# Chunked attention and a two-expert router on one core: the same operations in a new planned order, with a longer instruction fetch in the planner and one more dependency for turned rows

## Chip, cores and metric

The kernel runs on one core of one Trainium2 chip. The metric is device time in microseconds (us) of one execution. The core has TensorE (PE, matmuls and their weight loads), VectorE (DVE), ScalarE (ACT), GpSimd (POOL, which also issues most DMAs) and SyncE (SP, which issues DMAs only).

## What is computed

Attention in chunks, then a mixture of experts on its rows. The reference, cut to what matters:

```python
# q, k, v: (4, 8, 768, 64); mem_k, mem_v: 8 memory rows per head
for c in range(768 // 32):                       # chunks of 32 queries
    k_full = concat(mem_k, k[16 before .. 8 behind the chunk])   # 64 rows; v alike
    a = softmax(q_c @ k_full.T / sqrt(64))
    out[chunk] = a @ v_full
x = out as (3072 tokens, 512)
logits = x @ w_gate + log1p(exp(x @ w_noise)) * noise            # 8 experts
top2 = the two best experts of each token; weights by softmax over the two
for e in range(8):
    out[tokens of e] += weight * (relu(x @ w1[e]) @ w2[e])       # 512 -> 1024 -> 512
```

## The kernel before

**Attention.** A *pair* is two heads of one batch element (here a *batch* is one of the four batch elements, 768 tokens); there are 16 pairs, four to a batch, and a *group* is two pairs whose q, k and v are loaded together. The operations of a pair, with the planner's labels: `tq` and `tk` turn q and k on PE; `eq` and `ek` copy them out of PSUM; `sc` makes the scores; on DVE `mx` takes their maximum and `sb` subtracts it (L592, L608); `ex` is the exponential on ACT (L611); `tp` turns it, `ep` copies it; `pvo` multiplies it with v (L631); `rc` and `ml` divide by the sum and write the rows (DVE, L635 and L647); `tx` and `exx` turn the rows for the router. Loads are DMAs that GpSimd issues: `lq`, `lk` (one each a group) and `lv` (two halves a group). `lm`, on SyncE, copies the memory rows of v into the same tile. The memory rows' source, `memv`, lies inside the tile `XS`, which later holds the turned rows of the experts. There are 3 buffers each for q, k and v of a group, one PSUM tile for scores and one for outputs.

**Router.** After four pairs a batch is routed: `lg` makes the logits on PE (L693), `r1` is softplus on ACT, `r2` on DVE chooses two experts of each token (the choice, `pk`, L707 to L722), `r3` on PE ranks the tokens by matmuls with a triangle (L735 to L739), `r3s` and `r6` give each token a slot (L749 to L772), `r4`, `r5`, `r7` make the gates (L759 to L760, L763, L903 to L907), `r8` and `r8a` build one-hot products (`ohv` at L744, on DVE or POOL; `ohl` at L786), `r9` (L793) sums them to a table of token numbers by slot, `s0` to `s3` and `stab` do the same for spare slots. The rows and gates are written to memory (L913, on SyncE). The labels of batch 2 end in `_s`, those of batch 3 in `_l`.

**Experts.** There are 28 tiles of tokens, one for each two experts. For experts 0 and 1 half of each tile is *sealed* once batch 2 is routed: its token numbers are final (`gid_s`, L807), and 7 gathers (L949) fetch its rows. `tt` turns gathered rows on PE (L980), `xev` copies them into `XS` (L368 or L370), `fo` is the first matmul of an expert, one for each 128 columns of the hidden layer (L1055; `fo_a` for sealed halves), `relu` follows (L1065, L1067), `so` is the second matmul (L1096), DVE or ACT weights and adds it (L1105 to L1115), and POOL scatters the sum to the output (L1127). After attention the remaining PSUM banks serve the experts.

**What sets the order.** Every operation is given to a planner with a list of engines and durations, the operations that it depends on, its buffers and a priority. `Planner.run` plays the program through and writes each engine's instructions in the order of its own start times; each engine then runs its instructions strictly in that order on the chip, and waits on the chip come from the tiles that an instruction reads and writes, not from the planner's dependencies. `SHIFT` adds a number to the priority of an operation by label or by label and count. `FETCH` describes the fetch of PE's instructions: blocks of 128 products, the first edge at 94, and 6.3 us from the start of one block to the time when the next one is there as long as the planned time is under 97, later 3.2 us. These lines hold it:

```python
            if o.mm:
                for edge in range(block + FETCH[0], products + o.mm + 1, FETCH[0]):
                    at = est + dur * (edge - products) / o.mm
                    stall = max(0.0, begun + (FETCH[2] if at < FETCH[3] else FETCH[4]) - at)
```

## Time and profile before

| | |
|---|---|
| time, 3 runs | 337.85, 338.81, 338.9 us (median 338.81) |
| the profiled execution | 333.6 us, of which the span from first to last instruction is 332.1 |
| PE busy | 282.3 us (85%), 2972 matmuls |
| weight loads | 177.1 us (53%) |
| DVE, ACT, POOL busy | 159.8, 147.9, 131.3 us |
| granted PE clock, mean | 0.903 |

Times in a profile are those of one execution. A timeline row has its start, its length, engine, line, operation, output and inputs, shapes, and in brackets the idle time before it with what ended that. A row of groups has busy time and the mean in ns of one instruction, then the idle time before such instructions. PEq and the like are an engine's sequencer.

### The profile page before, as it was taken

Reading aid. Unit: us, or ns where it says so; the run is one execution under the profiler, and the core shown is the slowest. Engines: PE = TensorE matmul, PEld = TensorE weight load, DVE = VectorE, ACT = ScalarE, POOL = GpSimd, SP = SyncE. Lnnn points to the kernel's source line nnn. Section 1 sums busy time; section 2 is a strip of 40 time slices with the busy share of each in tenths; the row PEclk is TensorE's granted clock in tenths of the full one; section 3 lists DMA queues with packets and bytes.
Section 4 is the critical chain, followed back from the end, with each engine's and each line's share of the span. In section 5 each row is a group of like instructions: output and inputs, shape, how many; then the busy total and the mean of one; then the engine's idle time right before and its main releaser. Section 6 shows DMA issues by size and latency. Waiting matters only on the chain.

```text
span 332.1 us, 7279 instructions
## 1 busy us (share of the span) xinstructions
PE 282.3 (85%) x2972; PEld 177.1 (53%) x2972; DVE 159.8 (48%) x372; ACT 147.9 (45%) x261; POOL 131.3 (40%) x178
## 2 busy tenths in 40 slices
PE   0587588777567679999999999999999999999991
PEld 0575366665446456664646655545545744744540
DVE  7776677888748776824313431144042041043041
ACT  8675667888264134760611417403703604603500
POOL 7767533345000776987282410132032032051072
PEclk9999975978755558999999999999999999999998
DMA  7999999999999359289999910699613621021032
GB/s 100 208 128 139 149 150 149 212 171 195 223 183 116 89 127 177 79 140 188 247 210 227 248 68 0 106 182 198 101 54 78 99 79 57 2 109 51 3 122 82
DMA packets 80013, 43.55 MB, mean 131 GB/s; under 512 B 53805, under 2 KB 73262, under 8 KB 79974
## 3 DMA queue, kind: packets, MB, share of 16 engines
q0 software_dynamic: 74672, 38.78, 100.2%
q1 hardware_dynamic: 5014, 4.19, 4.9%
q8 instruction: 24, 0.39, 0.5%
q14 instruction: 15, 0.12, 0.1%
q10 hardware_dynamic: 288, 0.07, 0.1%
HBM read 61.26 MB, written 10.85 MB: 217 GB/s over the span
## 4 chain that ended last, share of the span: by engine, by line
PE 59%; DMA 21%; issue 8%; POOL 4%; DVE 4%; ACT 1%; POOLq 1%; DVEq 0%; ACTq 0%
PE ps_l L1055 20%; DMA vg<-in_v_dram 19%; PE ps_l L1096 18%; PE ps_g L1096 7%; PE ps_g L1055 7%; PE ps_l L980 2%; POOL out_dram L1127 2%; PE ps_o L631 2%; DMA kn<-in_k_dram 2%; PE ps_g L656 1%; DVE xrow L647 1%; POOL vg L516 1%; POOLq L1183 1%; PE ps_g L617 1%; PE ps_s L585 1%
## 5 line engine op out<-in xcount | busy, mean ns | idle before, releaser
L1065 ACT ACTIVATE ht<-ps_l 128x384 bf16<-128x384 f32 (+2 forms) x110 | 48.5, 491 | 95.0 <-PE ps_l L1055 94.0
L1096 PE MATMUL ps_l<-w2l,ht 128*128 128x512 bf16 x328 | 73.7, 379 | 0.0
L1096 PEld LDWEIGHTS <-ht 128*128 128x128 bf16 x448 | 43.6, 98 | 51.5
L1127 POOL DMA_INDIRECT out_dram<-acc,oid x28 | 28.8, 1028 | 84.9 <-DVE acc L1115 79.7
L1115 DVE SCALAR_TENSOR_TENSOR acc<-ps_l,gates,acc 128x512 f32<-128x512 f32 x22 | 16.5, 751 | 60.3 <-PE ps_l L1096 59.3
L1055 PEld LDWEIGHTS <-w1t 128*128 128x128 bf16 x416 | 31.4, 100 | 19.6 <-issue 2.2
L1055 PE MATMUL ps_l<-XS,w1t 128*128 128x384 bf16 (+4 forms) x312 | 40.7, 285 | 0.7 <-ACT XS L368 0.7
L1055 PEld LDWEIGHTS <-w1l 128*128 128x128 bf16 x320 | 29.9, 98 | 19.1
L1055 PE MATMUL ps_l<-XS,w1l 128*128 128x512 bf16 (+3 forms) x240 | 39.9, 316 | 0.0
L516 POOL DMA_DIRECT2D vg<-in_v_dram x18 | 23.7, 1317 | 23.3 <-DMA vg<-in_v_dram 10.7
L368 ACT COPY kT<-ps_q 64x768 bf16<-64x768 bf16 x31 | 24.6, 793 | 8.8 <-PE ps_q L555 8.2
L1096 PE MATMUL ps_g<-w2l,ht 128*128 128x512 bf16 x120 | 28.2, 379 | 0.0
L555 PE MATMUL ps_q<-identb,qn 128*64 128x128 bf16 x192 | 11.9, 276 | 15.6 <-POOL identb masks.py:199 10.6
L631 PE MATMUL ps_o<-vg,PT 128*32 128x132 bf16 x384 | 12.1, 279 | 9.0 <-DMA vg<-in_v_dram 5.0
L1107 DVE TENSOR_SCALAR acc<-ps_l,gates 128x512 f32<-128x512 f32 x13 | 9.8, 751 | 19.6 <-PE ps_l L1096 19.6
L1065 ACT ACTIVATE ht<-ps_g 128x384 bf16<-128x384 f32 (+2 forms) x38 | 16.8, 471 | 5.3 <-PE ps_g L1055 5.1
L949 POOL DMA_INDIRECT xl<-x_rows,gid x16 | 16.7, 1044 | 5.8 <-PE ps_l L980 2.2
L555 PEld LDWEIGHTS <-qn 128*64 128x64 bf16 x192 | 9.6, 147 | 16.6 <-DMA qn<-in_q_dram 12.6
L592 DVE TENSOR_REDUCE mx<-ps_s 128x12 f32<-128x768 f32 x16 | 15.3, 953 | 3.8 <-PE ps_s L585 3.4
L368 ACT COPY PT<-ps_g 128x768 bf16<-128x768 bf16 x13 | 10.3, 796 | 12.3 <-PE ps_g L617 11.2
L961 DVE COPY gates<-xl 64x8 f32<-64x8 f32 (+1 forms) x40 | 11.0, 292 | 9.9 <-DMA xl<-x_rows,gid 8.0
L647 DVE TENSOR_TENSOR xrow<-ps_o,rec 128x768 bf16<-128x768 f32 x16 | 15.3, 958 | 0.6
(179 smaller groups left out, 387.7 us busy)
## 6 DMA issues: line engine op xcount, KB each, us to landing
w2l<-in_moe_w_dram POOLq DMA_DIRECT2D x8, 1024.0 KB, 11.2
vg<-in_v_dram POOLq DMA_DIRECT2D x14, 336.0 KB, 20.9
w1t<-in_moe_w_dram POOLq DMA_DIRECT2D x4, 1024.0 KB, 22.3
w1l<-in_moe_w_dram POOLq DMA_DIRECT2D x4, 1024.0 KB, 10.5
kn<-in_k_dram POOLq DMA_DIRECT2D x8, 384.0 KB, 15.0
qn<-in_q_dram POOLq DMA_DIRECT2D x8, 384.0 KB, 18.7
x_rows<-xrow SPq DMA_DIRECT2D x2, 792.0 KB
x_rows<-xrow SPq DMA_DIRECT2D x2, 768.0 KB
```

Of the source, the lines that this page charges most:

```text
L368: A.copy(dst, src)
L516: G_.dma_start(out=vt[p0 + j:p0 + j + nj, hh, c:c + n, :D], in_=bass.AP(v.tensor, v.offset + (hd * S + c * chunk + j - left_ctx) * D, [[D, ...
L555: P_.transpose(out=dst.t[64 * hh:64 * hh + 64, t * QP:(t + 1) * QP], in_=s[:, j + 2 * hh, t, :], identity=identb)
L592: mx = op("mx", ("DVE", 0.98), lambda o, bmx=bmx, bS=bS: V.tensor_reduce(out=bmx.t, in_=sv(bS), axis=AX, op=Alu.max), deps=[sc], alloc=[bm ...
L631: P_.matmul(out=pvw[32 * r:32 * r + 32, u // UB, u % UB], lhsT=PT[:, u, 32 * r:32 * r + 32], rhs=vt[:, :, ncnk * j + c], start=True, stop= ...
L647: V.tensor_tensor(out=x5, in0=ov(bO)[:, :, :, :, :D], in1=r5.to_broadcast([128, 2, UB, 2, D]), op=Alu.mult)
L949: G_.indirect_dma_start(out=bx.t[:n], out_offset=None, in_=src, in_offset=bass.IndirectOffsetOnAxis(ap=ids_[:n, c:c + 1], axis=0), bounds_ ...
L1055: P_.matmul(out=dst, lhsT=w1b[e].t[:, kp, f * 128:(f + 1) * 128], rhs=src, start=(kp == 0), stop=(kp == KP - 1), skip_group_check=True)
L1065: A.activation(out=dst, in_=s_, func=Act.Relu)
L1096: P_.matmul(out=gy.t, lhsT=ht.t[:, f, j, :], rhs=w2b[e].t[:, f, :], start=(f == 0), stop=(f == FB - 1))
L1115: V.scalar_tensor_tensor(out=ba.t, in0=gy.t, scalar=gate, in1=ba.t, op0=Alu.mult, op1=Alu.add)
L1127: G_.indirect_dma_start(out=out_part[nv], out_offset=bass.IndirectOffsetOnAxis(ap=oid[:, c:c + 1], axis=0), in_=ba.t, in_offset=None, boun ...
```

## The change

Two lines and a table. `FETCH` has 6.9 in place of 6.3. The copies of turned rows, `xev`, have the last `lm` (`groups[-1][5][-1]`) as a further dependency, in both places where they are made; only the planner reads it. `SHIFT` is another table, of which one line stands here:

```diff
-FETCH = (128, 94, 6.3, 97.0, 3.2)
+FETCH = (128, 94, 6.9, 97.0, 3.2)
 SHIFT = {
-    "c_pool": 191.6, "c_smallv": 11.7, "c_wg": 69.7, "ek": 27.6, "ep": 29.4, "ep#0": 13.5, "ep#3": -50.3, "eq": 95.0, "eq#3": 26.1, "ex":
+    "c_mv": 74.6, "c_ones": 122.9, "c_smallv": 5.5, "c_wg": -72.5, "ek#27": 118.3, "ek#4": -17.2, "ep": 84.2, "eq#8": 49.7, "eq#9": 104.3,
...
-            ev = op("xev", DA(0.2 + w / 1900, 0.2 + w / 1250), xev, deps=[tt], use=[gx], prio=prio)
+            ev = op("xev", DA(0.2 + w / 1900, 0.2 + w / 1250), xev, deps=[tt, groups[-1][5][-1]], use=[gx], prio=prio)
...
-            ev = op("xev_a" if half == 0 else "xev", ("ACT", 0.2 + w / 1250) if half == 0 else DA(d_ + w / 1900, d_ + w / 1250), xev, deps=[tt], use=[gx], prio=prio)
+            ev = op("xev_a" if half == 0 else "xev", ("ACT", 0.2 + w / 1250) if half == 0 else DA(d_ + w / 1900, d_ + w / 1250), xev, deps=[tt, groups[-1][5][-1]], use=[gx], prio=prio)
```

The instructions are the same ones; on every engine they stand in another order, and some copies move between DVE and ACT. Line numbers after the change are two lower from the table on.

GpSimd's queue from the loads of group 4 to those of group 6, before (`qn` is q, `kn` is k, `vg` is v; `w1t` are the first weights of expert 0):

```order
L505 DMA qn2_94<-in_q_dram 128x4x384
L516 DMA vg1_99<-in_v_dram 56x48x64 x2
L505 DMA kn0_95<-in_k_dram 128x4x384
L505 DMA qn0_92<-in_q_dram 128x4x384
L516 DMA vg2_100<-in_v_dram 56x48x64 x2
L505 DMA kn1_96<-in_k_dram 128x4x384
L927 DMA w1t0_67<-in_moe_w1_dram 128x4x1024
L505 DMA qn1_93<-in_q_dram 128x4x384
L516 DMA vg0_98<-in_v_dram 56x48x64 x2
```

And after:

```order
L514 DMA vg1_99<-in_v_dram 56x48x64 x2
L514 DMA vg2_100<-in_v_dram 56x48x64
L742 TENSOR_TENSOR ohv_159<-pk_928,tnum_135 128x168
L514 DMA vg2_100<-in_v_dram 56x48x64
L925 DMA w1t0_67<-in_moe_w1_dram 128x4x1024
L503 DMA qn0_92<-in_q_dram 128x4x384
L503 DMA kn0_95<-in_k_dram 128x4x384
L503 DMA qn1_93<-in_q_dram 128x4x384
L503 DMA kn1_96<-in_k_dram 128x4x384
L514 DMA vg0_98<-in_v_dram 56x48x64 x2
```

`kn0` and `qn0`, k and q of group 6, stood ahead of v of group 5 (`vg2`) and now stand behind it and behind the weights; k and q of group 7 (`kn1`, `qn1`) stand together ahead of v of group 6. The hot-row product of batch 0 (`ohv`) has come from DVE into this queue, between the two halves of v of group 5; that of batch 1 now stands behind the last load of v. Earlier in the queue, k and q of group 3 and q of group 4 have moved behind v of groups 1 and 2.

DVE before, from the slots of batch 2 to the maximum of pair 14 (`rec` and `xrow` are the reciprocal and product of pair 12, `two` to the second `xrow` the gates of batch 2):

```order
L769 TENSOR_TENSOR pos<-ps_g_84,pk 128x168
L771 TENSOR_REDUCE at<-pos 128x6
L772 TENSOR_TENSOR slot<-at,fs 128x6
L635 RECIPROCAL rec_113<-ps_o_121 128x12
L647 TENSOR_TENSOR xrow_78<-ps_o_121,rec_113 128x6x2x64
L903 TENSOR_TENSOR two<-key,m_1932 128x48
L904 TENSOR_TENSOR ge<-ge,two 128x48
L905 TENSOR_REDUCE gs<-ge 128x6
L906 RECIPROCAL gs<-gs 128x6
L907 TENSOR_TENSOR xrow_80<-ge,gs 128x6x8
L778 SCALAR_TENSOR_TENSOR base_151<-ps_g_84,smin 128x28
L592 TENSOR_REDUCE mx_105<-ps_s_120 128x12
```

And after, up to the product of pair 12 (the two `mx`, `sd` are the maximum and subtraction of pairs 13 and 14):

```order
L747 TENSOR_TENSOR fl<-pk,flip 128x168
L749 TENSOR_REDUCE fs<-fl 128x6
L590 TENSOR_REDUCE mx_106<-ps_s_120 128x12
L606 TENSOR_TENSOR sd_108<-ps_s_120,mx_106 128x768
L767 TENSOR_TENSOR pos<-ps_g_85,pk 128x168
L769 TENSOR_REDUCE at<-pos 128x6
L770 TENSOR_TENSOR slot<-at,fs 128x6
L784 TENSOR_TENSOR ohl<-ramp,slot 128x768
L590 TENSOR_REDUCE mx_105<-ps_s_120 128x12
L606 TENSOR_TENSOR sd_107<-ps_s_120,mx_105 128x768
L633 RECIPROCAL rec_113<-ps_o_121 128x12
L645 TENSOR_TENSOR xrow_78<-ps_o_121,rec_113 128x6x2x64
```

The gates, the hot-slot product (`ohl`) and the maxima of pairs 12 to 14 now stand ahead of pair 12's reciprocal. Between the reciprocal of pair 11 and that of pair 12 stand, in this order: the slots of batch 1 with their `ohl`, a copy of turned rows, spare steps of batch 1, a copy of k, the choice of batch 2, more spare steps, maximum and subtraction of pair 12, the gates of batch 2, and then the rows above. On PE the turn of q of pair 12 now stands ahead of the product with v of pair 11.

ACT before, from the last softplus to the first `relu` (`XS` rows are copies of turned sealed rows, `ht` rows the relu):

```order
L699 ACTIVATE ns<-ps_g_84 128x48
L700 ACTIVATE ns<-ns 128x48
L368 COPY XS<-ps_g_85 128x4x2x64 x2
L763 ACTIVATE ge<-ge 128x48
L368 COPY XS<-ps_l_2323 128x4x2x64
L368 COPY XS<-ps_l_2323 128x4x64
L368 COPY XS<-ps_l_2325 128x4x2x64 x2
L368 COPY XS<-ps_l_2323 128x4x2x64
L1065 ACTIVATE ht_69<-ps_l_2327 128x3x2x64
```

And after:

```order
L697 ACTIVATE ns<-ps_g_85 128x48
L698 ACTIVATE ns<-ns 128x48
L366 COPY XS<-ps_g_84 128x4x2x64 x2
L366 COPY XS<-ps_l_2334 128x4x2x64
L366 COPY XS<-ps_l_2334 128x4x64
L761 ACTIVATE ge<-ge 128x48
L1063 ACTIVATE ht_69<-ps_l_2337 128x3x2x64
L1063 ACTIVATE ht_69<-ps_l_2337 128x64
```

Four turned gathers are copied ahead of the gates' exponential, where it was two. On PE, accordingly, two `tt` stand between the last logits and the rank `r3_l`, where it was one, and three `fo_a` stand between the rank and the table `r9_l`, where it was one. Further on, the second `tt` of late rows of expert 0 stands directly ahead of `fo0`, where two `fo_a` stood between them. On DVE six copies of gates (L961) stand ahead of the last choice, where it was four.

26 rows, old and new, of the table SHIFT are left out of this document.

## The prediction

> **What bounds the kernel now.** I read the page first, then busy time by stage, then the chain of work that ended last, and last the timelines of single engines around the place where attention ends.
>
> The page's slices of TensorE (PE), eight microseconds each, show an attention part that is never full and an expert part that always is:
>
> ```profile
> PE   0587588777567679999999999999999999999991
> PEclk9999975978755558999999999999999999999998
> ```
>
> Busy time by stage (columns: stretch, its length, then busy time of PE, weight loads, VectorE, ScalarE, GpSimd, with counts; granted clock; DMA share; GB/s) puts numbers on it:
>
> ```profile
> 49.00:82.00 33.00, 25.51 (x615) 21.08 (x613) 28.06 (x75) 27.12 (x38) 13.59 (x13) 0.76 2.14 181
> ...
> 99.00:117.00 18.00, 12.94 (x255) 10.52 (x248) 14.48 (x38) 5.77 (x8) 6.59 (x9) 0.50 0.83 112
> ...
> 128.00:325.00 197.00, 197.00 (x1253) 107.62 (x1251) 62.28 (x126) 70.74 (x159) 71.06 (x81) 1.00 0.57 118
> 325.00:332.10 7.10, 0.02 (x1) 0.00 (x0) 0.75 (x1) 0.00 (x0) 1.39 (x2) 0.78 0.18 66
> ```
>
> From 128 to 325 us PE is busy in all 197 us at full clock, and 7.1 us of tail follow. The change adds and removes no matmul, so this part is a block of fixed length, and only when it begins can move the end, unless the new order puts a hole into it. Before it, no engine is full; the chain says who is late:
>
> ```profile
> 71.15 27.49 DMA vg<-in_v_dram
> 98.68 0.85 PE ps_o L631 x18
> ```
>
> Up to 98.68 us the loads of v set the pace. PE waits for the last half of v of group 6 and then has four pairs of heads to finish. These rows of PE's and VectorE's timelines show the last of that (in brackets: idle time before the row, and what ended it):
>
> ```profile
> 99.58 0.23 DVE L635 RECIPROCAL rec<-ps_o 128x12 f32<-128x12 f32 x1 [2.27 <-PE ps_o L631]
> 109.47 0.23 DVE L635 RECIPROCAL rec<-ps_o 128x12 f32<-128x12 f32 x1 [0.41 <-PE ps_o L631]
> 116.03 0.73 PE L693 MATMUL ps_g<-wgn,xt 128*128 128x16 bf16 x21 [0.41 <-DVE xt L370]
> 116.61 1.01 PE L980 MATMUL ps_g<-identb,xl 128*128 128x128 bf16 x8
> 119.37 0.32 PE L735 MATMUL ps_l<-pk,upper 128*128 128x168 bf16 x1 [1.75 <-DVE pk L722]
> 121.78 1.65 PE L1055 MATMUL ps_l<-XS,w1t 128*128 128x384 bf16 x8 [0.67 <-ACT XS L368]
> ```
>
> The reciprocal of pair 12 starts at 99.58, that of pair 14 at 109.47, the last logits end at 116.76 (116.03 + 0.73), and the first expert matmul starts at 121.78. From there PE never stops. So the time is 121.78 us, plus the block, plus the tail.
>
> **The change part by part.** *The constant and the wait.* They act in the planner alone. The wait would matter only if a copy into XS could be due before the last copy of memory rows, which SyncE issues here, more than 40 us ahead of the first copy of turned rows (after 116.61):
>
> ```profile
> 74.22 1.29 SPq L535 DMA_DIRECT2D vg<-XS  x2
> ```
>
> So it costs nothing, with a cover of 40 us. The longer fetch is aimed at stalls like this one:
>
> ```profile
> 41.40 0.35 PE L631 MATMUL ps_o<-vg,PT 128*32 128x132 bf16 x11 [2.29 <-issue]
> ```
>
> Such stalls lie before 60 us, where the loads set the pace, so removing them is worth nothing either; the rows of 99 to 122 us above name other releasers.
>
> *The loads.* Issues on GpSimd, and below them the time from issue to landing of each (last column):
>
> ```profile
> 32.38 0.80 POOL L505 DMA_DIRECT2D kn<-in_k_dram  x1
> 51.30 0.76 POOL L505 DMA_DIRECT2D qn<-in_q_dram  x1 [0.73 <-DMA kn<-in_k_dram]
> 58.33 1.39 POOL L516 DMA_DIRECT2D vg<-in_v_dram  x1 [2.02 <-DMA vg<-in_v_dram]
> 59.71 0.78 POOL L505 DMA_DIRECT2D kn<-in_k_dram  x1
> 60.48 0.78 POOL L927 DMA_DIRECT2D w1t<-in_moe_w_dram  x1
> ```
>
> ```profile
> kn<-in_k_dram POOLq DMA_DIRECT2D x1, 384.0 KB, 18.6
> qn<-in_q_dram POOLq DMA_DIRECT2D x1, 384.0 KB, 21.5
> vg<-in_v_dram POOLq DMA_DIRECT2D x1, 336.0 KB, 20.6
> kn<-in_k_dram POOLq DMA_DIRECT2D x1, 384.0 KB, 22.1
> w1t<-in_moe_w_dram POOLq DMA_DIRECT2D x1, 1024.0 KB, 26.7
> ```
>
> Landings are thus 51.0 (k of group 4), 72.8 (q of 6), 78.9 (last v of 5), 81.8 (k of 7) and 87.2 (first weights): a load of k takes 2.9, the weights 5.4. Now q and k of groups 6 and 7 stand behind v of group 5 and the weights, and the four loads of v of groups 6 and 7 still come last. The bytes ahead of those four are the same, so the last v lands where it did, about 98.7 and 103.5. But q of group 6 lands at 78.9 - 2.9 (k of 6 no longer ahead) + 5.4 = 81.4 instead of 72.8, and PE, which runs in order, has the scores of pair 12 and everything up to the logits of batch 2 behind it. Two hot-row products (L744) also move to GpSimd, in front of loads. One that comes too early blocks them, as here after the loads:
>
> ```profile
> 95.06 0.47 POOL L744 TENSOR_TENSOR ohv<-pk,tnum 128x168 f16<-128x168 bf16 x1 [12.16 <-DVE pk L722]
> ```
>
> The first of the two needs the choice of batch 0. The last v of group 2 now lands four loads of q or k before 51.0, at 40 to 43, and the choice follows at about 47 (an estimate); the load behind the product went out at 58.33 and may now go out near 50. Even a wait of 12 us is covered, as loads are issued 18 to 27 us ahead: zero, and at worst a few microseconds.
>
> *VectorE before the last pairs.* Pair 11 now needs, after 81.4, three PE steps of 12, 6 and 24 matmuls; the last takes 0.85 (the chain's row, at half clock), and I give the others 0.85 and 0.7: 83.8. ScalarE's copies just keep up (first slow rival), so I take 84.3. From pair 11's reciprocal to pair 12's, VectorE now has all this in a row:
>
> ```profile
> L592 DVE TENSOR_REDUCE mx<-ps_s 128x12 f32<-128x768 f32 x16 | 15.3, 953 | 3.8 <-PE ps_s L585 3.4 <-PE ps_s L588 0.3
> L608 DVE TENSOR_TENSOR sd<-ps_s,mx 128x768 f32<-128x768 f32 x16 | 15.2, 952 | 0.3
> L647 DVE TENSOR_TENSOR xrow<-ps_o,rec 128x768 bf16<-128x768 f32 x16 | 15.3, 958 | 0.6
> 92.90 0.21 DVE L707 TENSOR_TENSOR nn<-ns,nz_all 128x48 f32<-128x48 f32 x1 [2.09 <-ACT ns L700]
> 96.43 0.33 DVE L769 TENSOR_TENSOR pos<-ps_g,pk 128x168 f32<-128x168 f32 x1 [0.52 <-PE ps_g L739]
> 97.16 0.16 DVE L772 TENSOR_TENSOR slot<-at,fs 128x6 int16<-128x6 int16 x1
> 100.73 0.20 DVE L903 TENSOR_TENSOR two<-key,m 128x48 f32<-128x48 f32 x1
> 101.74 0.21 DVE L907 TENSOR_TENSOR xrow<-ge,gs 128x48 f32<-128x48 f32 x1
> ```
>
> Three maxima and three subtractions of 0.95 (5.7), a reciprocal and product (1.2), batch 2's choice up to its slots (92.90 to 97.32 less the wait of 0.52: 3.9) and its gates (100.73 to 101.95: 1.2), batch 1's slots (an estimate of 1.4 from the same rows), two hot-slot products, two copies and the spare steps (estimate 3.8, from 0.2 to 0.95 each): 17.2. Pair 12's reciprocal comes at 101.5, where it came at 99.58: 1.9 later. From it to pair 14's took 9.9, with the gates, a maximum, a subtraction and the hot-slot product in between; now those are done, and between stand two products with v (2 x 0.96 + 0.23), one maximum, one subtraction, a copy and the ids: 5.4, plus handovers between PE, ScalarE and VectorE (0 to 1.7, taken as 1.0). Pair 14 comes at 107.9 against 109.47: **1.6 gained**, between 4.5 (the v of group 6 alone sets pair 12, and handovers cost nothing) and a loss of 2 (pair 11 late by as much as the 1.7 of handovers and the 1.9 together).
>
> *After the last logits.* The 7.3 us from pair 14's reciprocal to the logits' end hold the same steps. Then PE turned two gathered tiles (116.61), waited 1.75 for the choice, ranked from 119.37, turned two more, and waited 0.67 for their copy: 5.0. Now all four are turned before the rank, and the rank is followed at once by expert matmuls. That needs four gathers by then, and they start earlier; here they started behind the ids by two microseconds:
>
> ```profile
> 107.52 0.18 DVE L807 SCALAR_TENSOR_TENSOR gid_s<-ps_g,tab 128x28 int32<-128x28 f32 x1
> 109.75 1.17 POOL L949 DMA_INDIRECT xl<-x_rows,gid_s  x1 [14.22 <-DVE rec L635]
> ```
>
> The ids now follow pair 12's product, at about 103 (101.5 + 1.2 + 0.2), and the gathers at 104 to 105. From the logits' end to the rank it took 2.6 (116.76 to 119.37); I add 0.2 for two more gate copies ahead of the choice. The rank takes at most 1.0 (rank, turn and the 0.67 fill 119.37 to 121.78). 2.6 + 0.2 + 1.0 = 3.8, so **1.2 gained**, from 2.0 to nothing.
>
> *A hole in the block.* Before, two groups of sealed expert matmuls stood between the last turn of late rows and the first matmul that reads it; now none does. A copy like that at 121.78 showed 0.67 of wait: **0.7 lost**, from 0 to 1.0.
>
> Sum: 1.6 + 1.2 - 0.7 = 2.1 us off the span of 332.1, 330.0. That execution took 333.6 as a whole; the runs' median is 338.81, 5.2 above it, and I carry the difference over: 336.7.
>
> *The clock.* PE has half its clock for a while after it stops waiting:
>
> ```profile
> 121.78:127.40 5.62, 5.62 (x50) 3.98 (x50) 3.68 (x21) 1.48 (x4) 2.02 (x3) 0.50 0.89 106
> ```
>
> 5.6 us of full work at clock 0.50. I carry this over unchanged. The Trainium skill, "TensorE: Matmul & The Clock Gate", Part 1, says that the gate opens after one busy window of about 3.4 us which runs freely; by that rule it could open up to 2.2 us sooner, 1.1 us of time, 335.6. The trace agrees with it so far that 5.6 lies between one and two such windows.
>
> **The rivals.** *Clock up early.* In the new order PE has denser work between 88 and 117 us. If the clock is up when the experts begin, the 5.6 us at half clock shrink by 2.8: 333.9. For it: the page's clock digit is 9 again in the slice from 58 to 66 us. Against: 0.50 throughout 99 to 117. By the page of the skill named above one busy window there would do; no row here shows how busy is enough.
>
> *ScalarE late, slower.* Pairs 6 to 11 now start when q of group 3 lands, one load before the 51.0 of k of group 4, so 48.1, and must be through by 81.4. ScalarE has between them 26 copies, 6 exponentials and 4 short steps:
>
> ```profile
> L368 ACT COPY kT<-ps_q 64x768 bf16<-64x768 bf16 x31 | 24.6, 793 | 8.8 <-PE ps_q L555 8.2
> L611 ACT ACTIVATE P<-sd 128x768 bf16<-128x768 f32 x16 | 13.5, 846 | 1.3 <-DVE sd L608 1.3
> ```
>
> 26 x 0.793 + 6 x 0.846 + 1.0 = 26.7 us in 33, a busy share of 0.81; the kernel before reaches 27.12 of 33.00 in 49 to 82. There is no cover left: at a share of 0.74 it takes 36.1, pair 12 starts 3.6 late, and all behind it: 340.3. It decides below about 0.76, where the gain is used up.
>
> *The last pairs end as before.* If pair 14 still comes at 109.5, because the loads stretch or handovers take longer, only 1.2 - 0.7 remains: 338.3.
>
> **How the numbers follow.** About 0.3%, 1.0 us, is what a measurement of this kernel can tell from no change, so faster means below 337.8 and slower above 339.8. The forecast has 0.47 (its own bounds 334.5 to 338.8; 0.36 of it below 337.8), the early clock 0.15, late ScalarE 0.24 (0.22 of it above 339.8), the unchanged end 0.14 (0.02 on either side). Faster 0.36 + 0.15 + 0.02 = 0.53, same 0.11 + 0.02 + 0.10 = 0.23, slower 0.24. For 8 in 10 the range reaches from near the early clock's time, 333.5, to just past that of late ScalarE, 340.6.
>
> **What would show it.** Right: reciprocal of pair 12 after 100.5 and of pair 14 before 109, gathers by gid_s starting near 104 instead of 109.75, expert matmuls near 119 to 120, PE full to the end but for one short wait for XS. Wrong: pair 11's product with v later than 86, with ScalarE busy up to it; a clock of 1.00 when the experts start; or a hole in the expert block of over 1 us, which no step here holds.

## The result and the profile after

The kernel after took 338.15 us (median of 12 runs, 336.84 to 339.9), the kernel before, on the same chip, 338.29 (12 runs). The ratio is **1.0138** (95% interval 1.0102 to 1.0175): 1.4% slower. Nine of before's twelve runs lay at 337.85 to 340.6 and three at 332.66 to 334.17, and the ratio takes of before the three fast runs alone, so it differs from that of the medians. A second comparison, the run a_again below beside 29 runs of before, gave 338.84 against 334.92: 1.0109 (1.0066 to 1.0152). The profiled execution of after took 337.33 us with a span of 335.8; before's were 333.6 and 332.1.

The page's slices of PE and its clock:

```profile
PE   0876758772976679799999999999999999999991
PEclk9999777776585759999999999999999999999998
```

Slice 16 (134 to 143 us, counted from 0) shows a 7 inside the expert block, where before every slice is a 9. VectorE's timeline after, with the reciprocals of pairs 11, 12 and 14:

```profile
85.78 0.23 DVE L633 RECIPROCAL rec<-ps_o 128x12 f32<-128x12 f32 x1 [4.39 <-PE ps_o L629]
...
104.24 0.22 DVE L633 RECIPROCAL rec<-ps_o 128x12 f32<-128x12 f32 x1
...
111.46 0.23 DVE L633 RECIPROCAL rec<-ps_o 128x12 f32<-128x12 f32 x1 [0.31 <-PE ps_o L629]
```

Pair 12 comes 4.66 us later than before (99.58), with no wait ahead of it: VectorE was at work. Pair 14 comes 1.99 later. PE's timeline after, from the wait for q of group 6 to the first expert matmul:

```profile
83.33 0.85 PE L553 MATMUL ps_q<-identb,qn 128*64 128x128 bf16 x12 [4.72 <-DMA qn<-in_q_dram]
...
118.50 0.75 PE L691 MATMUL ps_g<-wgn,xt 128*128 128x16 bf16 x22 [0.21 <-DVE xt L368]
...
122.79 0.30 PE L733 MATMUL ps_l<-pk,upper 128*128 128x168 bf16 x1 [1.92 <-DVE pk L720]
...
123.54 2.65 PE L1053 MATMUL ps_l<-XS,w1t 128*128 128x384 bf16 x13
```

The logits end at 119.25 (before 116.76), the experts start at 123.54 (before 121.78). Behind that PE now waits three times, where it never did (the timeline's rows with a wait):

```profile
137.33 0.40 PE L978 MATMUL ps_l<-identb,xl 128*128 128x128 bf16 x4 [0.78 <-DMA xl<-x_rows,gid_b]
...
141.77 3.24 PE L1053 MATMUL ps_l<-XS,w1t 128*128 128x384 bf16 x32 [1.29 <-DVE XS L368]
...
149.02 0.62 PE L978 MATMUL ps_l<-identb,xl 128*128 128x128 bf16 x8 [0.72 <-DMA xl<-x_rows,gid_b]
```

Together these waits are 2.79 us. Two of the waits are for gathers. GpSimd's timeline says when gathers started, and the chain of work that ended last names what they waited for:

```profile
110.04 1.18 POOL L947 DMA_INDIRECT xl<-x_rows,gid_s  x1 [15.12 <-DVE sd L606]
...
122.29 0.97 POOL L927 DMA_DIRECT2D w2l<-in_moe_w_dram  x1
132.89 1.09 POOL L947 DMA_INDIRECT xl<-x_rows,gid_b  x1 [9.63 <-PE ps_g L1053]
```

```profile
98.44 10.47 DMA x_rows<-xrow
125.21 6.88 DMA x_rows<-xrow
```

The timeline's releasers (`sd`, `ps_g`) are not what the gathers waited for; the chain names the writes of gates (`xrow` to `x_rows`). Token numbers of late rows were there at about 129, the first late gather started at 132.89, because the write of batch 3's gates, issued at 125.21, had not landed. Last, PE from the first expert matmul to its last, after and before (length, busy time, clock):

```profile
123.54:328.70 205.16, 202.37 (x1307) 111.14 (x1303) 62.46 (x144) 78.31 (x174) 72.53 (x82) 0.99 0.56 116
```

```profile
121.78:325.02 203.24, 203.24 (x1304) 111.95 (x1303) 66.47 (x150) 72.62 (x163) 73.57 (x84) 0.99 0.58 118
```

So the 3.7 us of span are: start of the block +1.76, holes +2.79, work in the block -0.87; the tail is the same 7.1.

### The profile page after: what moved, and what is told of

The parts are those of the page before. It is cut to its first block, busy times and chain, and to the rows that moved or that the text cites. A ratio compares the mean times of both kernels' runs of the same rounds, so it can differ in the third digit from the quotient of the medians.

```text
span 335.8 us, 7295 instructions
## 1 busy us (share of the span) xinstructions
PE 281.5 (84%) x2972; PEld 175.9 (52%) x2972; DVE 154.8 (46%) x356; ACT 153.2 (46%) x275; POOL 132.1 (39%) x180
## 3 DMA queue, kind: packets, MB, share of 16 engines
q0 software_dynamic: 74672, 38.78, 101.2%
## 4 chain that ended last, share of the span: by engine, by line
PE 52%; DMA 23%; issue 9%; POOL 8%; DVE 5%; POOLq 1%; ACT 1%; DVEq 0%
PE ps_l L1094 19%; DMA qn<-in_q_dram 15%; PE ps_l L1053 15%; PE ps_g L1094 6%; PE ps_g L1053 5%; DMA x_rows<-xrow 5%; POOL xl L947 3%; PE ps_q L553 3%; DMA xl<-x_rows,gid_b 2%; POOL out_dram L1125 2%; POOL rest L950 1%; PE ps_l L978 1%; POOL vg L514 1%; PE ps_s L583 1%; DVE sd L606 1%
## 5 line engine op out<-in xcount | busy, mean ns | idle before, releaser
L1063 ACT ACTIVATE ht<-ps_l 128x384 bf16<-128x384 f32 (+2 forms) x115 | 50.9, 467 | 78.1 <-PE ps_l L1053 76.0
L1094 PE MATMUL ps_l<-w2l,ht 128*128 128x512 bf16 x336 | 75.6, 379 | 0.0
L1113 DVE SCALAR_TENSOR_TENSOR acc<-ps_l,gates,acc 128x512 f32<-128x512 f32 x21 | 15.8, 751 | 51.5 <-PE ps_l L1094 49.5
L1094 PE MATMUL ps_g<-w2l,ht 128*128 128x512 bf16 x112 | 26.3, 379 | 0.0
L366 ACT COPY kT<-ps_q 64x768 bf16<-64x768 bf16 x28 | 22.2, 793 | 7.1 <-PE ps_s L586 2.9
L959 DVE COPY gates<-xl 64x8 f32<-64x8 f32 (+1 forms) x40 | 12.3, 318 | 21.0 <-DMA xl<-x_rows,gid_b 11.1
L366 ACT COPY qT<-ps_q 128x768 bf16<-128x768 bf16 x16 | 12.8, 798 | 11.8 <-PE ps_q L553 11.5
L654 PE MATMUL ps_g<-identb,xrow 128*128 128x128 bf16 x96 | 12.2, 299 | 4.8 <-DVE xrow L645 3.4
L368 DVE COPY XS<-ps_l 128x256 bf16<-128x256 bf16 (+2 forms) x14 | 5.5, 421 | 23.0 <-PE ps_l L978 22.7
L1113 DVE SCALAR_TENSOR_TENSOR acc<-ps_g,gates,acc 128x512 f32<-128x512 f32 x7 | 5.3, 751 | 23.0 <-PE ps_g L1094 23.0
```

Of the source, the lines that this page charges most:

```text
L366: A.copy(dst, src)
L654: P_.transpose(out=d[:, u, :], in_=x4[:, u, 128 * i:128 * (i + 1)], identity=identb)
L959: V.tensor_copy(gates[rows, cc, :], bx.t[rows, XC:].bitcast(F32))
L1063: A.activation(out=dst, in_=s_, func=Act.Relu)
L1094: P_.matmul(out=gy.t, lhsT=ht.t[:, f, j, :], rhs=w2b[e].t[:, f, :], start=(f == 0), stop=(f == FB - 1))
L1113: V.scalar_tensor_tensor(out=ba.t, in0=gy.t, scalar=gate, in1=ba.t, op0=Alu.mult, op1=Alu.add)
```

## The experiments

My theory after the result had three parts: *loads* (q of group 6 and the last v land later, so the last pairs start late), *VectorE's row* (from pair 11 to pair 12 it works 18.5 us with 1.0 of waits in all), and *the DMA queues* (the small write of gates and the gathers stand behind the 1 MB load of expert 0's second weights). Rivals stand in each expectation. Labels that begin with b_ are the kernel before with an edit, the others the kernel after. Most edits move operations in the planned order by these lines (an operation by its label and its count, and the one that it is put behind); the added lines shift line numbers by some.

```diff
+    for label, count, behind in MOVES:
+        o = next(x for x in order if (x.label, x.num) == (label, count))
+        order.remove(o)
+        order.insert(next(i for i, x in enumerate(order) if (x.label, x.num) == behind) + 1, o)
```

**The mark.**

> The kernel after once more, with no change, as the mark for the three others on the same chip, since before took 338.3 us (median) in one comparison and 334.6 in another. Both theories: 336.8 to 339.9 if the kernel after does not depend on the chip; if it moves as before did, 334 to 336. In the profile the first late gather behind the write of gates again, 7 to 8 us behind its issue.

It took 338.84 us (337.99 to 340.02), with before at 334.92: after doesn't follow before to lower times on this chip. The first late gather came at 135.39, 9.2 us behind the write's issue (126.17). The other runs were timed in several comparisons, on different chips, each beside before; a ratio is always to before in its own.

### The last pairs

**Loads back.**

```diff
+MOVES = [("lq", 6, ("tk", 7)), ("lk", 6, ("tk", 7)), ("lv", 10, ("lq", 6)), ("lv", 11, ("lv", 10)),
+         ("lm", 5, ("lv", 11)), ("lk", 7, ("tk", 9)), ("o10", 0, ("lk", 7)), ("lq", 7, ("o10", 0))]
```

> The kernel after, with GpSimd's loads of groups 5 to 7 back in the order of before: q and k of group 6 ahead of v of group 5, k of group 7 ahead of the first weights. Load theory (pair 12 came at 104.24 because q of group 6 landed at 83.3 and VectorE then had 18.5 us of work in a row): q of group 6 lands at 72 to 77, pair 12's reciprocal at 100 to 102, that of pair 14 at 107 to 109, the last logits end near 116.5 instead of 119.25, and the time is 1.5 to 3 us shorter than the kernel after. Rival (VectorE's order itself, with gates, hot-slot product and maxima ahead of pair 12's reciprocal, is what costs; loads do not matter): pair 12's reciprocal stays later than 103.5 and the time within 0.7 us of the kernel after.

It took 336.77 us against 338.31 of before, ratio 0.9997 (0.9953 to 1.0041). VectorE's timeline of this run:

```profile
84.33 0.23 DVE L642 RECIPROCAL rec<-ps_o 128x12 f32<-128x12 f32 x1 [0.73 <-PE ps_o L638]
...
102.79 0.22 DVE L642 RECIPROCAL rec<-ps_o 128x12 f32<-128x12 f32 x1
```

Pair 11 and pair 12 both come 1.45 us earlier than in after: the row between them is 18.46 us in both. Neither side was right alone: the loads set when the row begins, VectorE how long it is. The loads gave 1.45 us alone because PE, no longer held by q of group 6, waited 4.06 us for v of group 5 instead (at 80.21). The logits ended at 117.66, and the three holes were there again (2.5 us).

**Pair 11 ahead of the waiting turn.**

```diff
+MOVES = [("tq", 12, ("r9", 1)), ("eq", 12, ("tq", 12))]
```

> The kernel after, with one step of PE moved: the turn of q of pair 12, at which PE waits 4.72 us for q of group 6, stands behind the work of pairs 8 to 11 and the slots of batch 1 that was queued behind it (pair 11's product with v, its turns, the rank and table of batch 1), and its copy on ScalarE moves along. Head-of-queue theory (pair 11 was ready at 80.1 and only stood behind the waiting turn, so that VectorE idled 4.39 us and then had 18.5 us of work in a row): pair 11's reciprocal at 81 to 82 instead of 85.78, pair 12's at 100 to 101.5 instead of 104.24, last logits' end 115.5 to 117 instead of 119.25, time 2 to 3.5 us below the kernel after. Rival (the order on VectorE between pair 11 and pair 12 costs, whatever comes before): pair 11 early, but pair 12 still later than 103 and the time within 0.7 us of the kernel after.

It took 336.33 us, ratio 1.0033 (1.001 to 1.0055). VectorE, and PE, of this run:

```profile
82.60 0.23 DVE L636 RECIPROCAL rec<-ps_o 128x12 f32<-128x12 f32 x1 [0.86 <-PE ps_o L632]
...
104.88 0.23 DVE L636 RECIPROCAL rec<-ps_o 128x12 f32<-128x12 f32 x1 [1.53 <-PE ps_o L632]
```

```profile
103.98 0.85 PE L632 MATMUL ps_o<-vg,PT 128*32 128x132 bf16 x24 [2.05 <-issue]
```

Pair 11 came 3.2 us earlier, pair 12 didn't, and the logits' end (119.65) was no earlier either. The time still lies 1.8 us below after's 338.15 in another comparison; this profile, with a span of 335.7, doesn't show where that comes from. The product with v waited 2.05 us for something the profile doesn't show; its `PT` had been copied at 101.9. The landing of that half of v is not recorded here; in a_again, with the same order of loads, it is (GpSimd's issue, then time from issue to landing):

```profile
73.79 1.39 POOL L516 DMA_DIRECT2D vg<-in_v_dram  x1 [1.12 <-DMA vg<-in_v_dram]
```

```profile
vg<-in_v_dram POOLq DMA_DIRECT2D x1, 336.0 KB, 30.5
```

It landed at 104.3, where before had 98.6. So v of group 6 is taken to be a second limit, close behind VectorE's; a_best (below) has such a wait with the landing beside it.

**Pair 12 earlier on VectorE**, with the loads back:

```diff
+MOVES = [... the eight of the loads ..., ("pvo", 12, ("ep", 12)), ("rc", 12, ("pvo", 12)), ("ml", 12, ("rc", 12))]
```

> The kernel after with the loads in the order of before (as in the run with the loads back) and, beside that, pair 12's product with v, its reciprocal and product ahead of the hot-slot product of batch 2 and of pair 14's maximum and subtraction. VectorE-order theory (18.5 us of work stand in a row between the reciprocals of pairs 11 and 12): pair 12's reciprocal at 100 to 101 instead of 102.79, pair 14's at 108 to 109 instead of 109.98, last logits' end near 116.3 instead of 117.66, 1 to 2 us shorter than with the loads alone. Rival (the work is only put behind; the handovers of the last pairs set the end): pair 12 early, pair 14 and the logits within 0.5 us of 109.98 and 117.66, no change.

It took 336.87 us, ratio 1.0044 (1.0012 to 1.0075); with the loads alone it was 336.77. VectorE's timeline:

```profile
102.15 0.23 DVE L645 RECIPROCAL rec<-ps_o 128x12 f32<-128x12 f32 x1 [2.71 <-PE ps_o L641]
108.40 0.23 DVE L645 RECIPROCAL rec<-ps_o 128x12 f32<-128x12 f32 x1 [0.58 <-PE ps_o L641]
```

Pair 12 waits 2.71 us for PE, whose v landed at 101.2, and what was put behind it delays pair 13 (6.25 us later instead of 3.6). The rival was right: the work is only put behind.

**The row write out of the way**, in after, in before, and with three edits (below):

```diff
+MOVES = [("rows_x_s", 0, ("rows_g_s", 0))]
```

> The kernel after, with the write of batch 2's rows (768 KB on SyncE, issued at 87.03) moved behind the write of batch 2's gates, so that it is issued near 98.9. Row-write theory (the last loads of v land late, at 100.8 to 104.3 where 98.7 was forecast, since this write runs beside them; 644 KB of its packets were counted from 92 to 96 us against 444 KB in before): the second half of v of group 6 lands 2 to 3 us earlier, at 98 to 101; in the kernel after VectorE's work still holds pair 12's reciprocal at 103 to 104, so the time changes by less than 1 us, unless the gathers, which wait for the write, start after 111. Rival (VectorE or the order of loads alone sets the landing): v of group 6 lands after 101 as before, no change.

> The kernel before, with the same write moved in the same way (issued at 86.50 before, near 102.4 then). In before PE waited 2.36 us at 98.68 for v of group 6 and VectorE was idle 2.27 us in front of pair 12's reciprocal. Row-write theory: v lands 2 to 3 us earlier, pair 12's reciprocal at 97 to 98, and the time is up to 2 us shorter, if the gathers (109.75) do not become later by more than they have slack. Rival: the write of 768 KB then lands near 110 to 112, the gathers of sealed rows start 1 to 3 us later, and PE waits for them behind the last logits: no gain or 1 to 2 us slower.

> The run with the three edits (loads back, gates first, second weights behind the write of gates), and beside that the write of batch 2's rows behind that of its gates. There pair 12's product with v waited 1.55 us for v of group 6, which landed at 102.80. Row-write theory: v of group 6 lands at 98 to 100.5, pair 12's reciprocal is then bound by VectorE at 102 to 102.8 instead of 103.79, 1 to 1.5 us shorter than the run with three edits. Rival: landing unchanged at 102 to 103, or the gathers later because the write now ends later, so that PE waits for rows of sealed tiles: no change or up to 2 us slower.

Landing of the first half of v of group 7 in the run in after, and of the second half of v of group 6 in the run in before (issue, then time to landing):

```profile
77.33 1.37 POOL L516 DMA_DIRECT2D vg<-in_v_dram  x1 [3.91 <-PE ps_o L631]
```

```profile
vg<-in_v_dram POOLq DMA_DIRECT2D x1, 336.0 KB, 23.4
```

```profile
72.01 1.39 POOL L518 DMA_DIRECT2D vg<-in_v_dram  x1
```

```profile
vg<-in_v_dram POOLq DMA_DIRECT2D x1, 336.0 KB, 25.2
```

They landed at 100.7 instead of 105.1 (a_again: issued at 78.38, 26.7 us), and 97.2 instead of 98.6: the 768 KB write does hold v. It gained nothing. In after VectorE still held pair 12 (104.54), the copies of gates on VectorE, which stand ahead of the last choice, waited 2.51 us for sealed gathers, and the time was 339.61 us, 1.0157 (1.0115 to 1.0198). In before pair 12 came at 98.14 and the logits ended at 114.84, but the gathers became the wait: 337.08 us, 1.0065 (1.0034 to 1.0095). With three edits it was likewise: pair 12 came at 102.08 and the logits ended at 115.99, and then, in PE's timeline,

```profile
119.45 0.61 PE L993 MATMUL ps_g<-identb,xl 128*128 128x128 bf16 x4 [3.02 <-DMA xl<-x_rows,gid_s]
```

This run took 334.65 us, ratio 1.0019 (0.9992 to 1.0047), no better than without the move (334.21).

### The write, the gathers and the weights

**The load of second weights moved**, behind the fourth late gather of after; in before ahead of the last sealed gather, or behind the third late one:

```diff
+MOVES = [("o20", 0, ("gather", 3))]
```
```diff
+MOVES = [("o20", 0, ("gather_a", 5))]
```
```diff
+MOVES = [("o20", 0, ("gather", 2))]
```

> The kernel after, with the load of expert 0's second weights moved on GpSimd from ahead of the gathers of late rows to behind the fourth of them; nothing else moves. Queue theory (the 1 MB load, issued at 122.29, stands in the DMA queues in front of the small write of batch 3's gates, issued at 125.21, and the gathers wait for that write): the first late gather starts when its token numbers are there, near 129.3 instead of 132.89; the waits of PE for gathers at 137.33 and 149.02 (0.78 + 0.72 us) go, the one for XS of 1.29 us at 141.77 may stay; PE's end and the time 1.0 to 2.0 us earlier. Rival (VectorE is late with the token numbers and that alone delays the gathers; the write is slow by itself): first gather still after 132, time within 0.5 us of the kernel after. A risk of its own: the weights come too late for the second matmuls, a new hole where they start.

> The kernel before, with the load of expert 0's second weights moved ahead of the last sealed gather, so that it is issued near 120.2 instead of 121.73 and thus ahead of the write of batch 3's gates at 121.08. Queue theory: the write then takes 6 to 8 us, the first late gather starts at 128 to 130 instead of 126.14, and holes come into the expert block, which had none: 1 to 2.5 us slower. Rival (the order of the load and the write is indifferent): gathers at 126.1, no change within 0.5 us.

> The kernel before, with the same load moved behind the third late gather, so that the write of gates has the DMA queues to itself. In the profile of before the gathers waited for their token numbers alone, and the write was issued 0.65 us ahead of the load. Queue theory: that profiled execution gains nothing (first gather at 126.1, time 333 to 334); if the 0.65 us are what separates before's executions near 333 from those near 338, all executions are now near 333. Rival (what separates them is the granted clock or something else): executions near 338 remain as frequent as for before.

They took 342.72, 340.0 and 341.8 us, ratios 1.0201 (1.0147 to 1.0255), 1.0111 (1.0055 to 1.0166) and 1.0205 (1.0147 to 1.0263). All three were slower, two of them against my expectation. In the first, GpSimd and PE:

```profile
131.52 1.02 POOL L949 DMA_INDIRECT xl<-x_rows,gid_b  x1 [7.83 <-DVE gid L807]
```

```profile
152.38 1.72 PE L980 MATMUL ps_l<-identb,xl 128*128 128x128 bf16 x12 [2.49 <-DMA xl<-x_rows,gid_b]
```

The first late gather now waits for its token numbers (`gid`), as the queue theory says, but the fifth and later ones stand behind two 1 MB loads (136.96 and 137.90). In the two kernels from before the write got ahead of the load (in b_w2_ahead too, where both were issued within 0.05 us: packets of the write 121.22 to 121.91, of the load from 122.03), so they don't test the write; the gather behind the load is the one that PE waits for:

```profile
130.54 0.61 PE L982 MATMUL ps_l<-identb,xl 128*128 128x128 bf16 x4 [4.71 <-DMA xl<-x_rows,gid_s]
```

```profile
138.51 0.40 PE L982 MATMUL ps_l<-identb,xl 128*128 128x128 bf16 x4 [3.94 <-DMA xl<-x_rows,gid_b]
```

In all three a gather close behind the load made PE wait, 2.49 to 4.71 us; in before the next gather was issued 4.4 us behind the load, and PE did not wait. The wait cost more than itself, for the granted clock fell behind it: it was 0.50 from 129.20 to 136.02 in b_w2_ahead, which takes another 3.4 us, and for 3.4 us, which takes 1.7, in the other two. The packets of the traces, counted by size, show the write itself:

```
                      write of batch 3's gates        load of 1 MB (1 KB packets)   first late
                      issued   768 packets of 32 B    issued   packets              gather
before                121.08   122.41 to 123.04       121.73   123.48 to 131.32     126.14
after                 125.21   129.00 to 131.56       122.29   123.97 to 131.37     132.89
a_w2_behind           126.55   127.45 to 127.97       136.96   138.67 to 146.68     131.52
a_w2_delay (below)    123.73   124.63 to 125.15       125.32   126.99 to 134.54     128.33
```

Ahead of the load the 24 KB take 0.5 to 0.6 us; behind it they end with it. The Trainium skill, "DMA: Bandwidth & Descriptors", section "Queues, rings and completion order", says that a DMA engine takes turns between queues, packet by packet; by that a write on another queue would be expected to move along beside a load. The trace of after agrees only in the write's last 2.6 us: for 3.8 us from its issue no packet of it moved, where 0.9 to 1.3 us passed in the rows ahead of the load. Why it stood is not shown.

**Choice and gates earlier.**

```diff
+MOVES = [("r8_l", 0, ("r4_l", 0)), ("r7_l", 0, ("r5_l", 0)), ("og", 1, ("r7_l", 0)),
+         ("og", 2, ("og", 1)), ("r3s_l", 0, ("r7_l", 0))]
```

> The kernel after, with VectorE's queue behind the last logits changed: four of the six copies of gates that stood ahead of the choice stand behind batch 3's gates, and the gates stand ahead of the token order (fl, fs). The choice comes 0.7 us and the write of gates about 1.2 us earlier, near 124.0. Queue theory (the 1 MB load, issued at 122.3, is still ahead of the write): first late gather at most 1 us earlier than 132.89, holes in the expert block still 2 to 3 us, time 0.3 to 0.9 us shorter through the choice alone. Rival (the write's own issue time counts): first gather 1.2 us or more earlier, holes below 1.5 us, time 1.5 us or more shorter.

It took 337.92 us, ratio 1.0087 (1.0054 to 1.0121). VectorE's and GpSimd's timelines:

```profile
122.63 0.21 DVE L908 TENSOR_TENSOR ge<-ge,two 128x48 f32<-128x48 f32 x1 [1.68 <-ACT ge L767]
```

```profile
132.94 1.09 POOL L953 DMA_INDIRECT xl<-x_rows,gid_b  x1 [9.77 <-PE ps_g L1059]
```

The choice came earlier, but the gates then waited 1.68 us for their exponential, which stands behind copies of turned rows on ScalarE, and those behind a turn on PE that waited 2.27 us for a sealed gather (at 121.17). So the write went out as long behind the logits' end as in after (117.61, 123.57), and the rank, behind the same turn, gained nothing from the earlier choice. The load (122.20) was still ahead of it, the gather came as late, and the holes were 2.72, as the queue theory has it.

**Expert 2's weights back behind the tenth gather.**

```diff
+MOVES = [("o12", 0, ("gather", 9))]
```

> The kernel after, with the load of expert 2's first weights moved from between the fourth and fifth late gathers to behind the tenth, where it stood before. Queue theory: the gathers behind it land sooner, the wait of 0.72 us at 149.02 goes, the other two holes (0.78 and 1.29) stay: 0.5 to 0.8 us shorter. Rival (the gathers are slow for their own sake, or behind expert 0's second weights): hole at 149 unchanged, no change.

It took 339.96 us, ratio 1.0142 (1.0103 to 1.0181), no better than after. The wait at 149 went, but PE waits later for the second weights of expert 1, now behind two loads in a row:

```profile
172.45 2.76 PE L1096 MATMUL ps_l<-w2l,ht 128*128 128x512 bf16 x11 [2.16 <-DMA w2l<-in_moe_w_dram]
```

**The load behind the write by idle time**, five fills in after, two in before:

```diff
-  lambda o: G_.dma_start(out=w2b[e].t, ...)
+  lambda o: ([G_.memset(rest, 0.0) for _ in range(5 if e == 0 else 0)], G_.dma_start(out=w2b[e].t, ...))
```

> The kernel after, with five idle fills of 0.55 us on GpSimd in front of the load of expert 0's second weights, so that it is issued near 125.9, behind the write of gates at 125.2 and ahead of the late gathers. Queue theory: the write lands within 1 us, the first late gather starts when its token numbers are there, near 129.5 instead of 132.89, the waits for gathers at 137.33 go, and the time is 1 to 2 us shorter than the kernel after. Rival (the gathers meet the same load, now 3.6 us later, and land no sooner): gathers start early but the holes of PE stay at 2 to 3 us in all, or move to the second matmuls: no change or slower.

> The kernel before, with two idle fills of 0.55 us on GpSimd in front of the load of expert 0's second weights, so that it is issued near 123.1, 2 us behind the write of gates instead of 0.65, and still 3 us ahead of the late gathers. If that margin is what separates before's executions near 334 from those near 338: all executions between 333 and 336. If not (rival: something earlier, or the granted clock): the same spread from 333.5 to 340.4, the median within 1 us of before's or above it, since the load now collides 1.4 us longer with the gathers.

In after it took 335.55 us (334.92 for before), ratio 1.0034 (1.0004 to 1.0063), **3.3 us below a_again on the same chip**, the largest gain of a single edit. GpSimd, and PE's only row with a wait in the expert block:

```profile
128.33 1.08 POOL L949 DMA_INDIRECT xl<-x_rows,gid_b  x1 [2.06 <-DVE gid L807]
```

```profile
139.54 3.24 PE L1055 MATMUL ps_l<-XS,w1t 128*128 128x384 bf16 x32 [0.64 <-DVE XS L370]
```

The waits for gathers are gone. Of the 5.3 us between the spans of the two profiles (338.5 and 333.2), 2.65 stand ahead of the first expert matmul (124.70 and 122.05), where the edit can do nothing. Behind it the holes went from 2.57 to 0.71, and 1.7 more went with a stretch of half clock behind a_again's holes (0.50 from 140.47 to 143.88). So in these two profiles holes and clock come to 3.6 us, about the gain in time. In before the fills gave 335.56 against 334.64, 1.0018 (0.9997 to 1.0038): no gain, two short waits for gathers (0.46 and 0.40).

### Together

**Loads back, gates first, two fills:**

> The kernel after with three edits: the loads back in the order of before, gates of batch 3 ahead of four copies of gates, and two idle fills of 0.55 us ahead of the load of expert 0's second weights, so that it goes out near 123.6, behind the write of gates near 122.3. If the three causes add up (loads 1.4, choice 0.4 to 1.2, write and gathers 1 to 2 us): 3 to 4 us shorter than the kernel after, 334 to 335, and level with before's fast executions or below them. If they overlap (rival: each only uncovers the next wait): 1.5 us or less below the kernel after.

It took 334.21 us against 334.92, ratio 0.9985 (0.9945 to 1.0024), 4.6 below a_again. The product of pair 12 with v, in PE's timeline:

```profile
102.89 0.85 PE L643 MATMUL ps_o<-vg,PT 128*32 128x132 bf16 x24 [1.55 <-issue]
```

v of group 6 landed at 102.8 (issued at 71.82, 31.0 us); the row write moved away (above, a_best_rows) took this wait off and gained nothing. **Four fills**, and then **the turn of late rows one step earlier** beside them:

```diff
+MOVES = [... the thirteen of the three edits ..., ("tt", 1, ("fo_a", 13)), ("xev", 2, ("xev", 1)), ("xev", 3, ("xev", 0))]
```

> The run with three edits, but with four idle fills instead of two ahead of the load of expert 0's second weights, so that it is issued near 125.4, 1 us behind the write of gates instead of 0.3 us ahead of it. Queue theory: the write never meets the load, the first late gather follows the token numbers at 129.3, executions lie within 332 to 335 where they spread from 332.2 to 337.6, the median 0 to 1 us lower. Rival (the spread comes from the loads of v or the clock): same spread and median.

> The run with four fills, and beside that the second turn of late rows one step of PE earlier: two sealed first matmuls of expert 1 stand between it and the first matmul that reads its copy, as in before, and the copies move with it. Handover theory: the wait of 0.64 us for XS goes, the rows are there (their gather landed 2 us ahead), time 0.6 us shorter than the run with four fills. Rival: the turn, now 1.6 us earlier, waits for its gather instead: no change.

They took 335.07 and **334.06 us**, against 337.51 for before in this comparison: 0.9946 (0.991 to 0.9982) and 0.9925 (0.9885 to 0.9964). The executions did not move together (333.36 to 338.96), so the fourth fill did not settle their spread. The last version has no wait of PE behind its first expert matmul:

```profile
121.34 2.98 PE L1070 MATMUL ps_l<-XS,w1t 128*128 128x384 bf16 x12
```

It is the fastest of all here; but before's median was 334.64 to 334.92 in three other comparisons, 0.2 to 0.3% above it, so that it beats before is shown for this comparison only.

## Why the prediction was wrong, step by step

| step | forecast | measured after |
|---|---|---|
| q of group 6 lands | 81.4 | 83.3 |
| reciprocal of pair 11 | 84.3 | 85.78 |
| VectorE from there to pair 12 | 17.2 | 18.46 |
| pair 12 to pair 14 | 6.4 | 7.22 |
| pair 14 to logits' end | 7.3 | 7.8 |
| logits' end to first expert matmul | 3.8 | 4.3 |
| first expert matmul | 119.0 | 123.54 |
| holes in the block | 0.7 | 2.79 |
| span | 330.0 | 335.8 |

The first five rows add 1.9 - 0.4 + 1.3 + 0.8 + 0.5 = 4.1 and the sixth 0.5: with rounding the 4.54 of the seventh. Holes add 2.09, the block's work takes off 0.87: 5.8, the whole error of the span.

So the steps that failed are three: the loads of group 6 were put too early, VectorE's row from pair 11 to pair 12 too short, and the gathers were taken to wait for token numbers alone, so that neither their late start nor the holes behind them had a term. Against before, the start of the block moved by +0.5 (pair 11), +4.1 (the row), -2.7 (pair 12 to 14), +0.5 (to the logits' end) and -0.7 (to the experts): the 1.76 above.

*The loads.* "So the last v lands where it did" failed: the second half of v of group 6, at 98.6 in before, landed at 104.3 in a_again and at 100.8 in a_gates_first, whose loads stand in after's order; in after itself it is not recorded, but the product with it started at 102.84. The forecast counted the bytes on GpSimd's queue and left out SyncE's, though the page lists both; moving the 768 KB row write brought v 1.4 us forward in before and 4.4 in after (2.0 against a_gates_first, where the same half landed at 102.7). As the write runs in both kernels, it can account for the difference of these figures at most, and single executions differ by as much. Why v landed later, and why q of group 6 missed its forecast by 1.9, stays open.

*VectorE.* The mechanism was right and its size was off by 1.3: of the 18.46 us it worked 16.18, against 8.00 of 14.32 in before. The pieces of the sum were not too short; the gaps between 45 instructions (1.3) and 1.0 of waits were missing. Rows of stretches, after and before:

```profile
85.78:104.24 18.46, 14.29 (x288) 11.78 (x288) 16.18 (x45) 12.16 (x18) 1.00 (x2) 0.68 1.94 185
```

```profile
85.26:99.58 14.32, 7.80 (x144) 6.58 (x145) 8.00 (x20) 6.69 (x11) 0.47 (x1) 0.55 2.04 196
```

The bound given for pair 14, a loss of 2, is what came true, partly by luck: it was worked out from pair 11 and the handovers, not from VectorE's gaps.

*After the logits.* "The gathers at 104 to 105" failed, with 110.04: the ids were there at 105.8, but the gathers also wait for the write of gates, issued at 98.44, 3.5 us earlier than before, and landed no earlier (last packet 108.47; before 108.20). The forecast took the ids as the gathers' only releaser; in before they started 2 us behind the ids, and that gap was the write: 1.55 us behind its last packet, 1.57 in after. The turns came ahead of the rank as forecast, but the choice began 1.41 us behind the logits' end instead of 0.55: six gate copies ran on VectorE until 120.57 and the softplus on ScalarE until 120.63. That is 0.86 us, where the forecast had 0.2 for the copies.

*The hole.* The handover was right: 0.64 us in a_w2_delay, a_best and a_best4, where it is the only wait left, 0.7 forecast, and the run that closed it was a microsecond faster (335.07 to 334.06, which their intervals don't separate). What no step held was the wait for gathers. The prediction's own sign of error, "a hole in the expert block of over 1 us", is what showed. The order of two issues on different queues had changed: the load 0.65 us behind the write before, 2.9 ahead of it after. The prediction did not look at GpSimd's and SyncE's issues around 121 together.

*The rivals.* ScalarE was not late: its last copy for pair 11 ended at 80.09, then it waited:

```profile
84.23 0.80 ACT L366 COPY qT<-ps_q 128x768 bf16<-128x768 bf16 x1 [4.14 <-PE ps_q L553]
```

So the loss came by another way than late ScalarE. That rival's price was off too: 48.1 + 36.1 is 84.2, which is 2.8 behind 81.4 and not 3.6. "Clock up early" came in half: after 123.54 the clock was 0.50 for about 2.1 us, before for 5.7. That alone takes 1.8 off the block, of which 0.87 was left; what used up the rest was not found. The clock rose at 127.53 in before and at 125.66 in after, and between the first and the last change of a trace it keeps each value for 3.41 us or a multiple of that, in all 19 profiles. Rows of the stretches ahead of the rise, before and after (length, PE's busy time first, clock behind the brackets):

```profile
120.70:124.12 3.42, 2.75 (x22) 1.99 (x22) 2.72 (x13) 0.86 (x2) 2.01 (x3) 0.50 0.45 63
124.12:127.53 3.41, 3.41 (x36) 2.38 (x34) 2.09 (x13) 1.39 (x3) 1.09 (x1) 0.50 1.08 126
```

```profile
122.25:125.66 3.41, 2.87 (x18) 1.86 (x18) 2.89 (x14) 0.59 (x3) 1.01 (x2) 0.50 0.53 83
```

The Trainium skill, "TensorE: Matmul & The Clock Gate", Part 1, has the clock rise after one busy window of about 3.4 us, and the windows run freely. Both traces agree: before's 5.7 us are the rest of one stretch with PE busy for 2.75, which did not do, and one full stretch; after's rank fell early enough into its stretch for 2.87 to do. Where work starts on this grid is luck, worth up to 1.7 us (an estimate, half of 3.41). The rule does not hold throughout: in a_loads_back PE was busy from 88.98 to 92.39 without a gap, a whole stretch of the grid, and the clock stayed at 0.50.

*The carry-over.* 5.2 us between before's profile and its runs were added as if they belonged to the program. After's runs lie 0.8 above its profile, so 336.7 came nearer to 338.15 than its steps deserved. What separates before's executions near 333 from those near 338 stays open: a later load (b_w2_delay) and a much later one (b_w2_behind) did not settle it.

## What to carry to other kernels

Where an order is replaced, list the issues of all queues by time, and for each small transfer ask which large one it has come to stand behind; a wait for a write can hide behind a wait for ids. A row of short instructions on an engine without gaps is a length to be summed with its gaps, and the engine's idle time before it tells nothing of its price. Of several late things the removal of one may give little: at pair 12 VectorE and v stood within 2 us of each other, and behind the logits choice and sealed gathers within 1 us. The one wait with nothing close behind it, the late gathers' for the write, gave most. A wait of PE can also cost half a clock for 3.4 us behind it, so holes are to be priced with the clock.

## What the runs showed of the hardware

- A 24 KB write of 32-byte packets on SyncE's queue took 0.5 to 0.8 us from first to last packet in the 11 profiles where it went ahead of a 1 MB load on GpSimd's queue; in the 8 where it stood behind the load its last packet came 6.0 to 8.1 us after its issue. In a_best the load was issued first, by 0.3 us, and the write still got ahead: its last packet ended at 125.92, the load's first started at 125.94.
- The same write for batch 2, issued between 96.1 and 103.6, ended from 108.1 to 110.0 in 13 of 19 profiles (105.3 to 111.5 in all): an earlier issue hardly brought an earlier end.
- The granted clock changed on a grid of 3.41 us. It fell to 0.50 for one or two steps behind PE's waits of 2.49, 3.94 and 4.71 us (a_w2_behind, b_w2_behind, b_w2_ahead) and behind two of 0.98 and 0.94 close together (a_again), but not behind those of 0.78 and 1.29 in after or 2.16 in a_w12_behind.
- With one and the same order, after and a_again differ by 2.7 us in the span (335.8 and 338.5): 1.2 at the first expert matmul (the sealed gathers start at 110.04 and 112.77) and 1.7 by the clock's fall. Differences below 1% between single profiles of this kernel mean nothing without the timed runs.
